# Constants made on chip, one buffer for the normalised values of batch 0, and a new written order, in a fused attention and mixing kernel

## The chip, the cores and the metric

The kernel runs on one core of a Trainium2 chip. The metric is the device time of one execution in microseconds (us); lower is better. The core has a matrix engine (TensorE, PE in the profile, with its weight loads as PEld), a vector engine (VectorE, DVE), an engine for activation functions (ScalarE, ACT), a general engine (GpSimd, POOL) and an engine that issues the transfers (SyncE, SP). Each takes its instructions in the order in which they are written; they wait for each other through semaphores.

## The reference

Four batches of 768 tokens, eight heads of 64. Every token attends to its neighbours at a distance under 16 and to 24 block summaries (the maximum of the keys and the mean of the values of 32 tokens); the result x goes through a gate with sine and cosine, is mixed over the tokens by two 768 by 768 matrices, and through a channel layer:

```python
    scores_l_m = np.where(mask_l, scores_l, -1000000000.0)
    scores_all = np.concatenate([scores_l_m, scores_s], axis=-1)
    scores_all = scores_all - np.max(scores_all, axis=-1, keepdims=True)
    a = np.exp(scores_all)
    a = a / (np.sum(a, axis=-1, keepdims=True) + 1e-09)
    ...
    theta = x @ w_theta
    cos_t, sin_t = (np.cos(theta), np.sin(theta))
    zr = x * cos_t
    zi = x * sin_t
    yr = np.einsum('ts,bsd->btd', w_tok_r, zr)
    yi = np.einsum('ts,bsd->btd', w_tok_i, zi)
    y = yr + yi
    u = x + y
    return (u + np.maximum(u @ w_ch, 0.0)).astype(np.float32)
```

## The kernel before, in words

The work is cut into 24 tiles of 128 tokens, six for each batch, counted here from 0 to 23. A tile goes through these stages, each with a letter that is used below:

- **S**, the scores (line 465, 32 matmuls into two PSUM banks `s`), then eight mask-and-minimum operations on VectorE (L501) and eight exponentials on ScalarE (L505);
- **PT**, the transposes of the exponentials (L514, two halves of four), each copied out of PSUM (L518);
- **AV**, the product with the values (L488, 32 matmuls); the rows are divided by their sums (L526 to L535) into a tile `xn`, three buffers of which go round;
- **X**, the transpose of `xn` (L544) into the one PSUM bank `t`, copied out (L294, L296) into `x`, the transposed x of the whole batch, which has two buffers;
- **TH**, the product with w_theta in four pieces (L569 for the first six tiles, with the weights as plain float32; L574 afterwards, with weights and x split into two parts) into the same bank `t`. The bank is free again when L583 on ScalarE and L587 on VectorE have read it;
- the phase: L583, L586, L587, an absolute value (L592 or L594), and sine and cosine (L598, L599) on ScalarE. Exponential and sine need different tables there, and each switch is an ACT_TABLE_LOAD;
- **Z**, the two products of `xn` with cosine and sine (L609), one for each half of the channels;
- **M**, the mixing (L637): for each batch and half of the channels six steps of four pieces, step i with the Z of tile i. The weights arrive as 64-bit words and are turned into float32 by L353 to L364 (ScalarE or VectorE, then GpSimd or VectorE, then three passes on VectorE).

Before the first tile, a pre-pass makes the block summaries: the maxima on VectorE (L392) and, for batch 0, the value sums as matmuls of `vn` (loaded into a buffer of the tag `x`) with a table of ones (L398). At the very beginning five matmuls on zeros (L331) keep TensorE running while the first transfers arrive. The last stage is the channel layer (L753) with its sums and outputs.

Nothing of the order is found at run time. The function records every operation with its inputs and outputs, and a long table of numbers, `ORDER`, says in which order they are written and which engine takes each (a letter behind the number: a for ScalarE, d for VectorE, g for GpSimd). Durations in the class `Program` and the `cost` of each operation were used when the table was searched; at run time only the table counts.

Three constants come from the host in one array `cst`: the identity for the transposes, three masks of 128 by 118, and the table of ones. They are loaded by three transfers into `cs` and `vt`.

Of the kernel before, what the change touches and what calls it, by code (L numbers as in the profile page):

```python
# [55 lines left out]
12 6d 14 0 13 15 4 7 8 28 18 9 10 11 3 16 20 1 22 19 33a 37g 35a 34a 39 38a 17 36a 40 41 49 5 52 56 42 44 43 46 50 54 47 74  # L56
75a 24 2 68 76d 51 45 53 48 55 170a 169a 21 23 25 26 59 57 164 29 31 27d 77 78 79 69d 70d 32d 71 72 30a 171 80 212 86 165
167 215g 216g 168g 58a 60a 172 175 176 179 173 174 178 81a 177 61 180 183 182 181 217 62a 184 187 185 186 65d 63 66 64d 67d
82g 166g 83 73 84 87a 188 190 199 88g 92 93 266 189a 191a 218 219 220 221 200a 192 224 223 270a 222 225 196a 193a 103a 213
214 94 95 89 85 90 226 91 194 227 197 229 230 228 195d 198d 231 233 232 269g 104g 108a 105 106 201 202 203 204 205 206d 207  # L60
234 236 271 245 235a 237a 109g 272 275 110 274 323a 276 279 246a 238 111 280 281 208a 242a 239a 278 285 284 320 268 322 267
96 389 97 98 321 99 100 101 102 107 112 113 114a 119a 282 240 273 283 243 241d 244d 277 287 286 247 248 249 250 251 115g
324g 116 117 252d 253 120g 209 288 325 290 299 300a 301 302 254a 289a 291a 292 326 118 255 121 210 122 211 123 258 303 256
# [892 lines left out]
```

## Time and profile before

| what | value |
|---|---|
| median of 3 runs | 454.6 us (454.58 to 455.56) |
| time of the profiled execution | 454.5 us |
| span of the instructions in it | 452.7 us |
| granted TensorE clock | 0.999 |
| busy: PE, PEld, DVE, ACT, POOL | 97%, 79%, 74%, 60%, 21% |
| table loads on ScalarE | 24 of 1283 ns |

The span runs from the first instruction to the last; what lies around it is 454.5 - 452.7 = 1.8 us. A row of the timeline gives the start, the duration, the engine, the line and the operation, how many follow each other, and in brackets how long the engine stood idle before it and what ended that. A row of the table of stretches gives the busy time of each engine in that stretch and how many instructions it began.

### The profile page before, as it was taken

The page shows a single profiled execution, that of the slowest core. Times are in us where ns is not written, and L with a number is a line of the kernel's source. Part 1 is how long each engine was busy: PE and PEld are TensorE (multiplying, and loading weights), DVE is VectorE, ACT ScalarE, POOL GpSimd, SP SyncE. Part 2 cuts the span into 40 slices and gives each one's busy share as a digit, 9 for nine tenths or more (in the row PEclk, how much of TensorE's full clock was granted, in tenths as well). Part 3 has the DMA queues.
Part 4 walks back from the last instruction along what each step waited for, and adds up shares of the span by engine and source line. Part 5 has one row for each costly group of instructions (what it writes and reads, how often), then busy time and mean ns, then how long its engine had stood idle before and what let it go on. Part 6 is the DMA issues. An engine that isn't in the chain of part 4 may idle for free.

```text
span 452.7 us, 9375 instructions
## 1 busy us (share of the span) xinstructions
PE 440.9 (97%) x3562; PEld 357.3 (79%) x3562; DVE 336.2 (74%) x930; ACT 271.9 (60%) x595; POOL 94.0 (21%) x98
## 2 busy tenths in 40 slices
PE   8888999999999999999999999999999999999997
PEld 3464655757888888888888888888888878999996
DVE  4799999778576576776638757575654599998996
ACT  2899988887774676966373755366664406526240
POOL 0221204635520103041011100012003100313521
PEclk9999999999999999999999999999999999999999
DMA  8999945323077340412710503101003720000256
GB/s 300 344 332 327 373 154 184 119 60 110 1 227 250 101 119 25 130 42 52 229 37 3 163 1 118 41 3 55 0 2 108 274 85 0 0 19 20 88 186 250
DMA packets 25005, 55.80 MB, mean 123 GB/s; under 512 B 2944, under 2 KB 8320, under 8 KB 24960
## 3 DMA queue, kind: packets, MB, share of 16 engines
q1 hardware_dynamic: 24960, 55.20, 37.4%
q8 instruction: 28, 0.46, 0.4%
q14 instruction: 17, 0.14, 0.1%
HBM read 45.75 MB, written 9.44 MB: 122 GB/s over the span
## 4 chain that ended last, share of the span: by engine, by line
PE 88%; DMA 8%; ACT 2%; DVE 1%; SPq 0%; issue 0%; ACTq 0%
PE m L637 46%; PE t L574 11%; PE c L753 6%; PE m L753 6%; PE pa L488 5%; PE s L465 4%; PE pa L514 4%; PE t L569 3%; DMA wt<-wti 3%; PE t L544 3%; DMA v<-vg 2%; DMA x<-vn 2%; DMA kn<-kT 1%; PE t L753 1%; ACT L598 1%; ACT w L598 0%
## 5 line engine op out<-in xcount | busy, mean ns | idle before, releaser
L637 PE MATMUL m<-wt,zh 128*128 128x512 f32 (+1 forms) x768 | 181.2, 360 | 0.8 <-DVE x L656 0.6
L637 PEld LDWEIGHTS m<-wt,zh 128*128 128x128 f32 x768 | 122.8, 189 | 32.8 <-issue 14.3
L637 PE MATMUL m<-wt,zl 128*128 128x512 f32 x336 | 86.6, 339 | 0.0
L505 ACT ACTIVATE e<-e,st 128x118 f32<-128x118 f32 x192 | 62.9, 388 | 16.3 <-DVE st L501 15.9
L637 PEld LDWEIGHTS m<-wt,zl 128*128 128x128 f32 x336 | 51.2, 188 | 7.4
L501 DVE CUSTOM_DVE_ANT_0 e<-s,cs 128x118 f32<-128x118 f32 x192 | 45.4, 273 | 10.7 <-PE s L465 6.8
L574 PE MATMUL t<-wth,xh 128*128 128x512 f32 x144 | 47.6, 412 | 0.0
L583 ACT ACTIVATE w<-t,bmagic 128x512 f32<-128x512 f32 x24 | 16.5, 688 | 42.2 <-PE t L574 41.3
L448 POOL COPY k<-kn 128x376 f32<-128x376 f32 (+1 forms) x24 | 12.7, 536 | 96.2 <-DVE zl L303 39.8
L488 PEld LDWEIGHTS pa<-v,e 118*64 118x64 f32 x768 | 24.7, 137 | 6.8 <-issue 4.2
L514 PEld LDWEIGHTS pa<-cs,e 128*118 128x118 f32 x192 | 22.7, 136 | 8.9 <-ACT e L505 1.6
L514 PE MATMUL pa<-cs,e 128*118 128x128 f32 x192 | 28.5, 274 | 0.8 <-ACT e L505 0.4
L488 PE MATMUL pa<-v,e 118*64 118x65 f32 x768 | 28.2, 224 | 0.8 <-ACT e L518 0.8
L574 PE MATMUL t<-wth,xl 128*128 128x512 f32 x72 | 28.3, 394 | 0.0
L465 PE MATMUL s<-k,q 64*64 64x118 f32 x768 | 25.3, 268 | 1.3 <-DVE st L527 0.7
L465 PEld LDWEIGHTS s<-k,q 64*64 64x64 f32 x768 | 19.7, 132 | 7.8 <-issue 5.9
L656 DVE TENSOR_TENSOR x<-m,x 128x512 f32<-128x512 f32 (+1 forms) x32 | 16.6, 548 | 11.6 <-PE m L637 11.6
L586 DVE TENSOR_SCALAR w<-w 128x512 f32<-128x512 f32 x19 | 8.6, 451 | 22.4 <-ACT w L583 22.3
L518 DVE COPY e<-pa 118x512 f32<-118x512 f32 x15 | 10.3, 688 | 18.9 <-PE pa L514 18.9
L574 PEld LDWEIGHTS t<-wth,xh 128*128 128x128 f32 x144 | 22.1, 189 | 2.7 <-DVE xl L550 0.3
L303 POOL TENSOR_TENSOR zl<-zb,zh 128x512 fp32r<-128x512 f32 x9 | 11.5, 1289 | 58.6 <-ACT zh L294 31.6
L587 DVE CUSTOM_DVE_ANT_0 w<-t,w 128x512 f32<-128x512 f32 x24 | 16.6, 690 | 8.0 <-POOL w L586 7.4
(168 smaller groups left out, 798.9 us busy)
## 6 DMA issues: line engine op xcount, KB each, us to landing
v<-vg SPq DMA_DIRECT2D x48, 195.0 KB, 4.5
q<-qg SPq DMA_DIRECT2D x24, 256.0 KB, 4.5
kn<-kT SPq DMA_DIRECT2D x6, 798.0 KB, 7.7
wt<-wtr SPq DMA_DIRECT2D x6, 768.0 KB, 10.1
wt<-wti SPq DMA_DIRECT2D x6, 768.0 KB, 11.9
f<-vT SPq DMA_DIRECT2D x12, 384.0 KB, 4.9
cu<-u_scratch SPq DMA_DIRECT2D x8, 384.0 KB, 6.4
out<-cu SPq DMA_DIRECT2D x16, 192.0 KB, 2.5
```

Of the source, the lines that this page charges most:

```text
L465: mm(0.79 * len(pairs) / NP, [lambda p=p, g=g, h=h: nc.tensor.matmul(sc[h].get()[ROW[g], p], q.get()[ROW[h], p, ROW[g]], k.get()[ROW[h], p ...
L488: mm(2 * 0.433 + scores[0] + (0.2 if scores[0] else 0.0), [lambda n=n, g=g, a=a: nc.tensor.matmul(xa[a].get()[ROW[g], n], turned[a].get()[ ...
L501: op({"DVE": 0.205}, lambda eng, n=n: nc.vector.tensor_tensor_reduce(e()[:, n], sc[n % 2].get()[:, 2 * a + n // 2], mask(m), -SCALE, 3.0e3 ...
L505: op({"ACT": 0.288}, lambda eng, n=n: nc.scalar.activation(e()[:, n], e()[:, n], AF.Exp, bias=st.get()[:, n:n + 1], scale=-1.0), [(st, n)] ...
L514: mm(NH * 0.109, [lambda n=n: nc.tensor.transpose(tp.get()[:NK, n], e()[:, n], ident()) for n in range(NH)], [e_ref, (cs, "ident")], [tp], ...
L544: mm(NC * 0.109, [lambda c=c: nc.tensor.transpose(tx.get()[:, c], xn[b, i].get().rearrange("p h d -> p (h d)")[:, c * P:(c + 1) * P], ident())
L574: calls = [lambda t=t, xx=xx, k=k, c=c: nc.tensor.matmul(th.get(), xx.get()[:, c], w_th[c].get()[:, k], start=(c == 0 and t == 0), stop=(c ...
L583: op({"ACT": 0.59}, lambda e: nc.scalar.activation(r(), th.get(), AF.Identity, bias=bmagic.get(), scale=1.0 / TWO_PI), [th, bmagic], [R], due)
L587: op({"DVE": c_dve(DM)}, lambda e: nc.vector._custom_dve(TENSOR_ADD_SAT, out=r(), in0=th.get(), in1=r(), s0=PI_F, s1=-PI_F), [th], [R], due)
L637: nc.tensor.matmul(acc[th](), zz.get()[:, r, cc], w[:, TT[th]], start=(s == 0 and r == 0 and t == 0 and (th == 0 or c == 0)), stop=(s == N ...
L656: op({"DVE": c_dve(nt * P)}, lambda e, u=u, acc=acc: nc.vector.tensor_tensor(u(), acc(), u(), op=ALU.add), [areg] + [(xs, n) for n in rang ...
L753: calls = [lambda k=k, t=t, x=x, y=y: nc.tensor.matmul(to.get(), weights[n][x][0]()[:, k, j * P:(j + 1) * P], operands[n].get()[:, y, k], ...
```

## The change

It has three parts. The lines behind the new code move by 34 to 36: the scores are L499 in the changed kernel, the products with the values L524, the transposes L550 and L580, the first products with w_theta L605, the mixing L673.

First, the constants are made on the chip. The three transfers go; in their place stand six fills (MEMSET, on VectorE or GpSimd) and seven AFFINE_SELECTs on GpSimd, which overwrite what lies off a line or a diagonal:

```diff
-    dma(lambda: sums.get().rearrange("p a n -> p (a n)")[:, :2 * NB - BPT], lambda: cst[:, P + 3 * NK:], (2 * NB - BPT) * 512, [], [sums], 1e6)
-    for k, c in (("mask", slice(P, P + 3 * NK)), ("ident", slice(0, P))):
-        dma(lambda c=c: cs.get()[:, c], lambda c=c: cst[:, c], (c.stop - c.start) * 512, [], [(cs, k)], 1e6)
...
+    def fill(dst, value, n, wr):
+        op({"DVE": c_dve(n, "fast"), "POOL": c_pool(n, False)}, lambda e: V[e].memset(dst(), value), [], [wr], -100.0, port=BOTH)
+
+    def keep(dst, pattern, n, base, step, compare, value, wr):
+        op({"POOL": c_pool(n, False) + 0.1}, lambda e: nc.gpsimd.affine_select(
+            out=dst(), in_=dst(), pattern=pattern, compare_op=compare, fill=value, base=base, channel_multiplier=step), [], [wr], -100.0, port=BOTH)
...
+    fill(lambda: masks(every, slice(0, NB)), math.log(BLK) / SCALE, 3 * NB, (cs, "mask"))
+    fill(lambda: masks(every, slice(NB, NK)), 0.0, 3 * NL, (cs, "mask"))
+    for g in range(2):
+        local = lambda g=g: masks(slice(g * QT, (g + 1) * QT), slice(NB, NK))
+        keep(local, [[0, 3], [1, NL]], 3 * NL, 0, -1, ALU.is_ge, far, (cs, "mask"))
+        keep(local, [[0, 3], [-1, NL]], 3 * NL, 2 * HALO, 1, ALU.is_ge, far, (cs, "mask"))
...
+    fill(flags, 1.0, 2 * NB - BPT, sums)
+    keep(flags, [[-BLK, 2 * NB - BPT]], 2 * NB - BPT, BLK * (NB - BPT), 1, ALU.is_ge, 0.0, sums)
+    keep(flags, [[BLK, 2 * NB - BPT]], 2 * NB - BPT, BLK - 1 - BLK * (NB - BPT), -1, ALU.is_ge, 0.0, sums)
+    fill(lambda: cs.get()[:, 0:P], 0.0, P, (cs, "ident"))
+    keep(lambda: cs.get()[:, 0:P], [[-1, P]], P, 0, 1, ALU.not_equal, 1.0, (cs, "ident"))
```

Second, the six `xn` of batch 0 become six parts of one buffer of the tag `x` (`Part` is a view of a slice; `early` holds the buffer). The tag still has two buffers. The first tile's `vn` has one, `early` the other, the transposed x of batch 0 takes the first one when the sums over `vn` are done, and the transposed x of batch 1 takes that of `early`, when the last Z of batch 0 has read it:

```diff
-        xn[b, i] = Ref(apool, [P, H, D], tag="xn", bufs=K["XNB"])
+        if b == 0 and i == 0:
+            early.append(Ref(tpool, [P, NT, H, D], tag="x", bufs=K["XB"]))
+        xn[b, i] = Ref(apool, [P, H, D], tag="xn", bufs=K["XNB"]) if b else Part(early[0], lambda x, i=i: x[:, i])
```

Third, the table `ORDER` is another one, searched with other durations; a line of each, and one of the durations:

```diff
-12 6d 14 0 13 15 4 7 8 28 18 9 10 11 3 16 20 1 22 19 33a 37g 35a 34a 39 38a 17 36a 40 41 49 5 52 56 42 44 43 46 50 54 47 74
...
-        op({"ACT": 0.16, "DVE": 0.19}, lambda eng: (
+        op({"ACT": 0.16, "DVE": 0.075}, lambda eng: (
```

What the table moves is seen in the order of the built programs, at three places. The first is the opening. On TensorE before, the five matmuls on zeros, the scores of tile 0 (`s`), the sums over `vn` (`x,vt`) and the transposes of tile 0:

```order
L331 MATMUL t<-zb 128x512 x5
L465 MATMUL s_110<-k,q 64x118
...
L398 MATMUL pa_164<-x,vt 24x512 x6
L514 MATMUL pa_173<-cs,e 118x128 x4
L514 MATMUL pa_178<-cs,e 118x128 x4
L465 MATMUL s_200<-k,q 64x118
...
L488 MATMUL pa_247<-v,e 64x65 x8
L488 MATMUL pa_256<-v,e 64x65 x8
L465 MATMUL s_271<-k,q 64x118
```

and now:

```order
L365 MATMUL t<-zb 128x512 x4
L432 MATMUL pa_120<-x,vt 24x512 x2
L499 MATMUL s_129<-k,q 64x118
...
L432 MATMUL pa_120<-x,vt 24x512 x4
L550 MATMUL pa_185<-cs,e 118x128 x4
L550 MATMUL pa_190<-cs,e 118x128 x4
L499 MATMUL s_222<-k,q 64x118
...
L524 MATMUL pa_265<-v,e 64x65 x8
L524 MATMUL pa_274<-v,e 64x65 x8
L365 MATMUL t<-zb 128x512
L499 MATMUL s_300<-k,q 64x118
```

A third of the sums over `vn` now stands ahead of the first scores, and the fifth matmul on zeros behind the first product with the values. GpSimd's first work, which was one copy of keys, is now this (`cs` holds masks and identity, `vt` the table of ones, `k` the keys of a tile; the ISA row is a reload of its library, which stood ahead of the first TENSOR_SCALAR before):

```order
L333 ISA
L333 AFFINE_SELECT vt<-vt 128x44
L330 MEMSET cs 128x3x94
L333 AFFINE_SELECT cs<-cs 64x3x94 x3
L333 AFFINE_SELECT vt<-vt 128x44
L333 AFFINE_SELECT cs<-cs 64x3x94
L330 MEMSET cs 64x15
L482 COPY k<-ks 128x4x24
L482 COPY k<-kn 128x2x94 x3
L482 COPY k<-ks 128x4x24
L482 COPY k<-kn 128x4x94 x2
L333 AFFINE_SELECT cs<-cs 128x128
```

Five of the six copies of keys for tile 0 are now on GpSimd, behind the masks. The second place is ScalarE around the second tile, before (L353 begins the conversion of a piece of w_theta when it has arrived, L518 copies the transposes of tile 1, L294 the transposed x of tile 0):

```order
L505 ACTIVATE e<-e,st 128x118 x4
L353 ACTIVATE xl<-wth_222 128x512
L518 COPY e<-pa_307 118x512
L518 COPY e<-pa_312 118x512
L294 COPY x<-t 128x4x128
```

and now:

```order
L541 ACTIVATE e<-e,st 128x118 x4
L482 COPY k<-kn 128x4x94
L554 COPY e<-pa_322 118x512
L554 COPY e<-pa_327 118x512
L387 ACTIVATE xl<-wth_218 128x512
L305 COPY x<-t 128x4x128
```

The two copies, for which the product AV waits, moved ahead of the conversion. The third place is TensorE where batch 1 begins to overlap the end of batch 0, before (the rows from the transposes of tile 7 to the last mixing step of batch 0's first half; `t<-cs,xn` is X of tile 6, `t<-wth` its TH, `m` the mixing):

```order
L514 MATMUL pa_1138<-cs,e 118x128 x4
L514 MATMUL pa_1143<-cs,e 118x128 x4
L544 MATMUL t<-cs,xn 128x128 x4
L465 MATMUL s_1162<-k,q 64x118
...
L488 MATMUL pa_1188<-v,e 64x65 x8
L488 MATMUL pa_1197<-v,e 64x65 x8
L574 MATMUL t<-wth_911,xh 128x512 x2
L574 MATMUL t<-wth_911,xl 128x512
L574 MATMUL t<-wth_846,xh 128x512 x2
...
L637 MATMUL m_664<-wt,zh 128x512
```

and now:

```order
L550 MATMUL pa_1147<-cs,e 118x128 x4
L550 MATMUL pa_1152<-cs,e 118x128 x4
L499 MATMUL s_1157<-k,q 64x118
...
L580 MATMUL t<-cs,xn 128x128 x4
L524 MATMUL pa_1192<-v,e 64x65 x8
L524 MATMUL pa_1201<-v,e 64x65 x8
L673 MATMUL m_646<-wt,zh 128x512
L673 MATMUL m_648<-wt,zh 128x256
...
L610 MATMUL t<-wth_774,xh 128x512 x2
```

The scores of tile 8 moved ahead of X of tile 6, and TH of tile 6, of which three pieces stood ahead of the mixing, now begins behind its third piece. Over the whole program ScalarE has 32 table loads instead of 24; the eight more all stand behind the first piece of the second half of batch 0's mixing. The numbers of matmuls of each kind are the same.

More of the change, by code (lines that the diff above doesn't have):

```diff
@@ L146, in get, with __init__ @@
         return self.ap
+class Part:
+    def __init__(self, base, cut):
+        self.base, self.cut = base, cut
+    def get(self):
+        return self.cut(self.base.get())
 class Late:
@@ L197, in op @@
                 ref, key = acc if isinstance(acc, tuple) else (acc, None)
[L198 to L206 removed]
+                own = ref.base if isinstance(ref, Part) else ref
+                if isinstance(own, Ref) and own not in o.refs:
+                    if not own.users:
+                        o.allocs.append(own)
+                        self.tags.setdefault((id(own.pool), own.tag), [[], 0])[0].append(own)
+                    else:
+                        first.add(own.users[0])
+                    own.users.append(o)
+                    own.left += 1
+                    o.refs.append(own)
                 st = self.state.setdefault(ref, {})
@@ L264, with attn_moe @@
             T_LEAD=30.0, Z_LEAD=14.0, PRE=2.0, START=34.82, W_LEAD=20.0, WT_LEAD=5.0)
-def attn_moe(tc, qg, vg, kT, vT, vn, wth, wtr, wti, wch, cst, out, tune=TUNE):
+def attn_moe(tc, qg, vg, kT, vT, vn, wth, wtr, wti, wch, out, tune=TUNE):
     nc = tc.nc
@@ L314, in attn_moe @@
     bmagic = Ref(wpool, [P, 1], tag="bmagic")
-    dma(lambda: sums.get().rearrange("p a n -> p (a n)")[:, :2 * NB - BPT], lambda: cst[:, P + 3 * NK:], (2 * NB - BPT) * 512, [], [sums], 1e6)
-    for k, c in (("mask", slice(P, P + 3 * NK)), ("ident", slice(0, P))):
-        dma(lambda c=c: cs.get()[:, c], lambda c=c: cst[:, c], (c.stop - c.start) * 512, [], [(cs, k)], 1e6)
+    masks = lambda rows, cols: cs.get()[rows, P:].rearrange("p (m k) -> p m k", k=NK)[:, :, cols]
+    flags = lambda: sums.get().rearrange("p a n -> p (a n)")[:, :2 * NB - BPT]
+    def fill(dst, value, n, wr):
[3 more added lines that the diff above has]
+            out=dst(), in_=dst(), pattern=pattern, compare_op=compare, fill=value, base=base, channel_multiplier=step), [], [wr], -100.0, port=BOTH)
+    every, far = slice(0, P), -1e9 / SCALE
+    pr.key = ("CONST", 0)
+    fill(lambda: masks(every, slice(0, NB)), math.log(BLK) / SCALE, 3 * NB, (cs, "mask"))
[4 more added lines that the diff above has]
+        keep(local, [[0, 3], [-1, NL]], 3 * NL, 2 * HALO, 1, ALU.is_ge, far, (cs, "mask"))
+    fill(lambda: masks(slice(0, QT), slice(NB, NB + HALO))[:, 0], far, HALO, (cs, "mask"))
+    fill(lambda: masks(slice(QT, P), slice(NB + HALO + QT, NK))[:, 2], far, HALO, (cs, "mask"))
+    fill(flags, 1.0, 2 * NB - BPT, sums)
[3 more added lines that the diff above has]
+    keep(lambda: cs.get()[:, 0:P], [[-1, P]], P, 0, 1, ALU.not_equal, 1.0, (cs, "ident"))
+    pr.key = ("", 0)
     bright = Ref(wpool, [P, 1], tag="bright")
@@ L933, in _layout @@
         "wch": con(moe_w_ch).view(np.int64).reshape(NC, P, DM),
-        "cst": _const(),
     }
```

188 lines of the change are left out of this document (84 added, 104 removed).

## The prediction

> **What bounds the kernel now.** The page gives TensorE 97% of the span, so I first looked for where the other 3% lies. The table of stretches shows it (start and end; then length and the busy time, with the instructions begun, of PE, PEld, DVE, ACT, POOL; granted clock, DMA share, GB/s):
>
> ```profile
> 0.00:50.00 50.00, 43.70 (x388) 23.72 (x389) 39.99 (x146) 37.89 (x89) 10.18 (x20) 1.00 0.99 329
> 50.00:80.00 30.00, 30.00 (x156) 17.52 (x155) 29.53 (x54) 25.84 (x50) 7.92 (x7) 1.00 0.63 218
> 80.00:110.00 30.00, 28.48 (x318) 19.33 (x318) 23.50 (x90) 24.41 (x61) 14.20 (x18) 1.00 0.30 89
> 110.00:345.00 235.00, 234.97 (x2117) 199.71 (x2117) 152.43 (x500) 145.53 (x336) 36.21 (x40) 1.00 0.26 79
> 345.00:400.00 55.00, 54.38 (x307) 47.99 (x306) 43.85 (x71) 21.01 (x33) 10.46 (x8) 1.00 0.29 98
> 400.00:449.00 49.00, 49.00 (x284) 48.94 (x283) 46.16 (x75) 17.20 (x29) 15.02 (x8) 1.00 0.30 109
> 449.00:452.70 3.70, 0.38 (x3) 0.06 (x1) 0.72 (x2) 0.00 (x0) 0.00 (x0) 0.82 0.61 218
> ```
>
> PE is idle for 6.30, 0, 1.52, 0.03, 0.62, 0 and 3.32 us, 11.8 in all. The last 3.32 are the final sum and its transfer, which nothing in the change touches. So this change can win at most 8.5 us, nearly all of it before 110 us, or lose wherever it makes TensorE wait anew. The full stretch from 50 to 80 is a warning: VectorE is busy there for 29.53 of 30 us.
>
> Then the timeline of PE before 46 us, only the rows at which it waits or changes stage (start, duration, engine, line, operation, count, idle time before and its releaser):
>
> ```profile
> 1.46 7.61 PE L331 MATMUL t<-zb 128*128 128x512 f32 x10 [1.46 <-DVE zb L329]
> 10.25 0.63 PE L465 MATMUL s<-k,q 64*64 64x118 f32 x16 [0.61 <-ACT k L448]
> 10.81 3.61 PE L398 MATMUL pa<-x,vt 128*24 128x512 f32 x8
> 14.77 1.90 PE L398 MATMUL pa<-x,vt 128*24 128x512 f32 x4 [0.34 <-DMA x<-vn]
> 16.60 1.40 PE L514 MATMUL pa<-cs,e 128*118 128x128 f32 x8
> 20.95 1.16 PE L465 MATMUL s<-k,q 64*64 64x118 f32 x32 [0.71 <-DVE st L527]
> 24.48 1.46 PE L488 MATMUL pa<-v,e 118*64 118x65 f32 x32 [0.82 <-ACT e L518]
> 31.78 0.65 PE L544 MATMUL t<-cs,xn 128*128 128x128 f32 x4 [0.37 <-DVE w L587]
> 37.71 0.54 PE L514 MATMUL pa<-cs,e 128*118 128x128 f32 x3 [0.41 <-ACT e L505]
> 40.04 0.66 PE L544 MATMUL t<-cs,xn 128*128 128x128 f32 x4 [0.24 <-DVE w L587]
> 41.88 1.12 PE L569 MATMUL t<-xh,x 128*128 128x512 f32 x2 [1.18 <-ACT x L294]
> 44.88 1.34 PE L637 MATMUL m<-wt,zh 128*128 128x512 f32 x3
> ```
>
> **The constants.** The three transfers that go carry little, by the list of DMA issues (KB each, median us to landing):
>
> ```profile
> x<-vn SPq DMA_DIRECT2D x3, 512.0 KB, 7.2
> q<-qg SPq DMA_DIRECT2D x24, 256.0 KB, 4.5
> kn<-kT SPq DMA_DIRECT2D x4, 399.0 KB, 5.0
> cs<-cst SPq DMA_DIRECT2D x1, 177.0 KB, 6.7
> cs<-cst SPq DMA_DIRECT2D x1, 64.0 KB, 7.9
> vt<-cst SPq DMA_DIRECT2D x1, 22.0 KB, 4.6
> ```
>
> 263 KB at 329 GB/s are 0.8 us of transfers, and three issues fewer on SP's queue. The fills on VectorE stand in its gaps before the first keys. The trace has no AFFINE_SELECT. The nearest rows on GpSimd, and the groups of the later steps:
>
> ```profile
> L448 POOL COPY k<-kn 128x376 f32<-128x376 f32 x23 | 12.3, 544 | 87.7 <-DVE zl L303 39.8 <-DVE zb L609 16.3 <-PE s L465 15.1
> L303 POOL TENSOR_TENSOR zl<-zb,zh 128x512 fp32r<-128x512 f32 x9 | 11.5, 1289 | 58.6 <-ACT zh L294 31.6 <-DVE w L609 21.5 <-DVE zh L296 4.8
> L501 DVE CUSTOM_DVE_ANT_0 e<-s,cs 128x118 f32<-128x118 f32 x192 | 45.4, 273 | 10.7 <-PE s L465 6.8 <-PE pa L514 2.3 <-PE pa L488 0.6
> L364 DVE SCALAR_TENSOR_TENSOR xl<-wth,xl 128x512 uint32<-128x512 uint32 x2 | 1.4, 689 | 0.0
> ```
>
> Scaled to 282 elements (3 masks of 94), one select or fill costs 0.41 us by the copy and 0.71 by the two-input operation. GpSimd has five such and three short ones (0.1 to 0.35 each). Begun at 1.5 us, when the fills that they overwrite are through, they end between 3.9 and 6.1. I take the middle, 5. The first to need `vt` are the sums over `vn` at about 8.0, so 2 to 4 us of waiting for transfers cover it: cost zero. Without that cover, by an end after 8.0, every us over is a us on the opening.
>
> **The opening.** TensorE is released by arrivals in both kernels. The last keys of tile 0 stood behind 1874 KB (four of 399, 256, 22); now four of 399 and one third of `vn` make 2108. The 234 KB more are 0.7 us, so the second half of the scores moves from 10.25 to 10.95. `q` now follows them; it is 490 KB behind what had landed by about 8.8, so near 10.3. In the time ahead of that a third of the sums over `vn` (12 matmuls took 3.61 + 1.90) is done, from about 8.0, when four of the five matmuls on zeros are through (five end at 1.46 + 7.61 = 9.07), to 9.9. Scores end at 11.6 instead of 10.9, and 3.7 us of sums remain: the transposes of tile 0 start at 15.3 instead of 16.60, as the wait of 0.34 for `vn` goes too (a piece of w_theta and the masks no longer stand ahead of its last third). But this lead of 1.3 isn't kept. The scores of tile 2 waited 0.71 until VectorE had done the eight masks of tile 1; these now start 1.3 earlier, yet two conversion passes (L364 is 0.69, L359 shorter) now stand among them. I expect 20.4 against 20.95, a lead of **0.55**.
>
> **From 20 to 80 us.** AV of tile 1 waited 0.82 at 24.48 for two copies that stood behind a conversion which itself waited for its weights:
>
> ```profile
> 23.24 0.67 ACT L353 ACTIVATE xl<-wth 128x512 f32<-128x512 f32 x1 [0.75 <-DMA wth<-wth]
> 21.00 0.61 POOL L357 TENSOR_SCALAR xh<-xh 128x512 f32<-128x512 f32 x1 [0.41 <-ACT xh L353]
> ```
>
> Now the copies go first: the wait goes whole, and the lead is 0.55 + 0.82 = 1.4. The waits 0.37, 0.41, 0.24 and 1.18 are 2.2 more, so at the first mixing step the lead could be 3.6. I don't give it all. What stands late next is VectorE: by the rows of the order, four masks (4 x 0.273 = 1.1 us), two conversion passes (1.4) and two divisions more lie ahead of the Z of tile 2, about 3 us with the smaller operations, and between 50 and 80 us VectorE has half a us to spare. How much of that a gap absorbs the trace can't say, so I let half of the 3.6 go there: the lead comes out at **1.8** for everything before 80 us. Bounds: 0, if VectorE takes it all; 4.8, if every wait but the first 1.46 goes (6.30 - 1.46).
>
> **Where batch 1 begins.** The rows from 94 to 104 us are one chain, TH of tile 5 to the first Z that the mixing step waits for:
>
> ```profile
> 94.94 0.69 ACT L583 ACTIVATE w<-t,bmagic 128x512 f32<-128x512 f32 x1 [0.26 <-PE t L569]
> 96.87 0.66 PE L544 MATMUL t<-cs,xn 128*128 128x128 f32 x4 [1.09 <-DVE w L587]
> 98.72 1.28 ACT L598 ACT_TABLE_LOAD   x1
> 99.51 0.74 PE L574 MATMUL t<-wth,xh 128*128 128x512 f32 x2
> 101.29 0.69 DVE L609 TENSOR_TENSOR zh<-xn,w 128x512 f32<-128x512 f32 x1 [0.40 <-ACT w L599]
> 102.04 4.14 PE L637 MATMUL m<-wt,zh 128*128 128x512 f32 x12 [0.19 <-DVE zh L609]
> 365.56 0.73 PE L637 MATMUL m<-wt,zh 128*128 128x256 f32 x3 [0.62 <-DVE x L656]
> ```
>
> The scores of tile 8 (32 such are 1.16 in the row at 20.95) now fill the wait of 1.09. The price is in the second edit: the copy of X of tile 6 into the transposed x of batch 1 must wait for the last Z of batch 0 (which follows the one at 101.29), because that buffer holds `xn`; bank `t` stays taken, and the three pieces of TH of tile 6 (from 99.51, about 2.1 us) that hid sine and cosine can't stand ahead of the mixing. One piece of the mixing step before (a third of 4.14, 1.4) takes their place. So TensorE has 0.7 us less to do inside the chain, and the chain stays at about 7.1 (102.04 - 94.94); it is shorter, down to 6.4, if the table load no longer stands behind the copies of tile 6. So what is won in front is lost behind: **0**, bounds -1.5 and +0.8. Queued behind the waiting copy on ScalarE are its exponentials for tile 8, and for those TensorE's next transposes.
>
> **The rest.** The wait at 365.56 shrinks as more pieces stand ahead of it: **-0.2** (bounds -0.6, 0). The turns between matmul kinds are 256 instead of 276 in the order; by the rows each costs or saves under 0.1 us, both signs, and I count zero. Eight more table loads on ScalarE lie between 110 and 345 us, where there were these:
>
> ```profile
> L598 ACT ACT_TABLE_LOAD x9 | 11.5, 1283 | 0.1
> L505 ACT ACT_TABLE_LOAD x8 | 10.3, 1283 | 1.7 <-DVE st L501 1.5
> ```
>
> 8 x 1.283 = 10.3 us on an engine that idles for 235 - 145.5 = 89 there, while TensorE waited 0.03 in spite of 17 loads. Cost zero, hidden under matmuls; 10.3 if the cover were gone at each.
>
> Sum against the profiled execution, 454.5 (span 452.7 and 1.8 around it; the median is 454.6): 454.5 - 1.8 + 0 - 0.2 = **452.5 us**.
>
> **Rivals.** *VectorE takes the whole lead.* For it: 29.53 of 30. Against: ten idle us on it before 50, into which the work moved forward goes. Then only the 0.2 stays: 454.3.
>
> *More is won.* Every wait goes before 80 and the one before the mixing: 4.8 + 0.2, about 449.5. Against: the new masks and conversions are in the way by the order itself.
>
> *Table loads on the chain (slower).* Place: the phases of batches 1 to 3. The load at 98.72 did stand on the chain to the mixing, between copy and cosine. If three of the eight new ones do so with no matmul ready, 3 x 1.283 = 3.85, and the time is 456.3. It decides from the third on (454.5 + 1.4 is passed by 2.7 loads). Against: 17 were hidden.
>
> *The library arrives late.* GpSimd's reload stands ahead of its first select now, and before ahead of the TENSOR_SCALAR at 21.00, which waited 0.41 and for ScalarE, so the reload cost no more there. If it stalled for long at the start, with the dear price, masks end at 9.7 to 11.1; the key copies behind them (four, 1.3 us) put the scores at 11.0 to 12.4, 1.4 late in the middle: 453.9. In the Trainium skill, "GPSIMD Engine Reference", section 2.1 on instruction dispatch, the first call to a freshly loaded kernel pays about 6 us without a visible instruction, which would give such an end; the 0.41 in this trace speaks against it.
>
> **The numbers.** Forecast, with its own range 450.5 to 453.1 (4.0 to 1.4 won): 0.57. More won: 0.06. VectorE takes it: 0.17. Library: 0.05. Table loads: 0.15. About 0.3%, 1.4 us, is what a measurement here can tell. So faster 0.63, same 0.22, slower 0.15. Range 449.9 to 455.6: up past the two cases of no change and down to most of the larger gain.
>
> **What would show it.** Right: transposes of tile 0 near 15.3, scores of tile 2 near 20.4, no wait at AV of tile 1, less than 4.5 us of PE idle before 50, still full from 50 to 80; selects of 0.4 to 0.7 us, over by 6.1; PE idle near zero from 110 to 345 with 25 loads. Wrong: new waits of PE on `xn`, `w` or `e` between 50 and 345 us, a mixing step that starts later than 102, or first scores after 11.

## The result, and the profile after

The changed kernel took 459.87 us (median of 6, 459.54 to 461.82), the kernel before on the same chip 454.91 us (median of 6). The ratio is 1.0104, with a 95% interval of 1.0084 to 1.0125: the change makes the kernel slower by about 5 us. The forecast was 452.5, with a range up to 455.6. The profiled execution of the changed kernel took 459.54 us with a span of 457.7; that is 5.0 more span than before (452.7), with the same 1.8 around it. The ratios of this document leave out two executions that took far longer than the others of their kernel, one of 1111.51 us (the run below that moves only the second sum) and one of 460.36 us (the kernel before).

The table of stretches of the changed kernel, at the cuts of the prediction (start and end; then length and the busy time, with instructions begun, of PE, PEld, DVE, ACT, POOL; granted clock, DMA share, GB/s):

```profile
0.00:50.00 50.00, 44.65 (x424) 24.41 (x425) 41.02 (x152) 37.81 (x88) 13.74 (x33) 1.00 0.99 334
50.00:80.00 30.00, 28.86 (x122) 16.12 (x121) 28.59 (x57) 23.00 (x43) 4.99 (x7) 1.00 0.50 175
80.00:110.00 30.00, 28.09 (x296) 19.61 (x297) 24.16 (x87) 24.78 (x62) 16.62 (x20) 1.00 0.42 115
110.00:345.00 235.00, 232.03 (x2119) 198.07 (x2116) 152.17 (x493) 154.86 (x346) 33.89 (x39) 0.99 0.25 79
345.00:400.00 55.00, 53.99 (x302) 46.83 (x301) 41.69 (x66) 21.92 (x34) 7.01 (x6) 1.00 0.27 96
400.00:449.00 49.00, 49.00 (x284) 48.93 (x283) 45.39 (x75) 15.43 (x27) 20.79 (x13) 1.00 0.23 82
449.00:457.70 8.70, 5.21 (x31) 4.89 (x29) 4.75 (x9) 0.95 (x2) 1.03 (x1) 1.00 0.74 267
```

PE is now idle for 5.35, 1.14, 1.91, 2.97, 1.01, 0 and 3.49 us, 15.9 in all, against 11.8 before. That is 4.1 of the 5.0 us; the other 0.9 is busy time (441.8 against 440.9), though the matmuls are the same. The opening won 0.95 us of idle time. Every stretch from 50 to 400 lost some, and by far the most was lost where before there was nothing to lose: from 110 to 345 us, 2.97 against 0.03.

The timeline of PE in the changed kernel, only rows at which it waits or changes stage (start, duration, engine, line, operation, count, idle time before and its releaser):

```profile
1.53 5.45 PE L365 MATMUL t<-zb 128*128 128x512 f32 x8 [1.53 <-DVE zb L363]
10.06 1.35 PE L499 MATMUL s<-k,q 64*64 64x118 f32 x32 [1.25 <-POOL k L482]
14.89 1.40 PE L550 MATMUL pa<-cs,e 128*118 128x128 f32 x8
18.44 1.15 PE L524 MATMUL pa<-v,e 118*64 118x65 f32 x30 [0.92 <-DMA v<-vg]
21.02 1.04 PE L499 MATMUL s<-k,q 64*64 64x118 f32 x32 [0.38 <-DVE x L571]
...
66.40 0.63 PE L580 MATMUL t<-cs,x 128*128 128x128 f32 x4 [0.36 <-DVE w L623]
72.52 9.30 PE L673 MATMUL m<-wt,zh 128*128 128x512 f32 x28 [0.77 <-DVE zh L645]
...
86.47 1.16 PE L499 MATMUL s<-k,q 64*64 64x118 f32 x32 [0.84 <-DVE st L537]
99.78 2.85 PE L673 MATMUL m<-wt,zh 128*128 128x512 f32 x8 [0.70 <-DVE zh L645]
...
239.95 0.73 PE L673 MATMUL m<-wt,zh 128*128 128x256 f32 x3 [2.22 <-DVE x L692]
240.52 0.76 PE L673 MATMUL m<-wt,zl 128*128 128x512 f32 x2
241.08 1.05 PE L610 MATMUL t<-wth,xh 128*128 128x512 f32 x2
241.94 0.63 PE L610 MATMUL t<-wth,xl 128*128 128x512 f32 x1
242.36 1.48 PE L673 MATMUL m<-wt,zh 128*128 128x512 f32 x4
243.64 0.69 PE L673 MATMUL m<-wt,zl 128*128 128x512 f32 x2
244.18 0.85 PE L673 MATMUL m<-wt,zh 128*128 128x512 f32 x4
244.87 0.51 PE L673 MATMUL m<-wt,zl 128*128 128x512 f32 x2
245.22 0.62 PE L610 MATMUL t<-wth,xh 128*128 128x512 f32 x2
245.67 0.40 PE L610 MATMUL t<-wth,xl 128*128 128x512 f32 x1
...
370.18 0.74 PE L673 MATMUL m<-wt,zh 128*128 128x256 f32 x3 [0.96 <-DVE x L692]
```

One wait stands out: 2.22 us at 239.95, for the sum of the mixing on VectorE (L692). And behind it the matmuls are slow. Four mixing pieces take 1.48 at 242.36 and 0.85 at 244.18; two pieces with w_theta 1.05 at 241.08 and 0.62 at 245.22. Over the five rows from 240.52 to 243.64, each against its like from 244.18 on, that is 0.25 + 0.43 + 0.23 + 0.63 + 0.18 = 1.72 us. The table of stretches for PE alone (busy time, clock, DMA share, GB/s) has the reason, the granted clock:

```profile
240.00:244.00 4.00, 4.00 (x13) 0.58 0.00 0
```

So in this execution this place costs 2.2 of waiting and 1.7 of slow clock, 3.9 of the 5.0 us. Why the sum came late is seen in VectorE's timeline of the changed kernel at that place,

```profile
235.56 0.76 DVE L571 TENSOR_TENSOR xn<-pa,st 128x256 f32<-128x256 f32 x2
236.23 1.74 DVE L426 TENSOR_REDUCE ks<-kn 128x48 f32<-128x1536 f32 x1
237.89 0.68 DVE L692 TENSOR_TENSOR x<-m,x 128x512 f32<-128x512 f32 x1
238.49 0.68 DVE L314 TENSOR_TENSOR zl<-w,zh 128x512 fp32r<-128x512 f32 x1
239.08 0.27 DVE L537 CUSTOM_DVE_ANT_0 e<-s,cs 128x118 f32<-128x118 f32 x1
...
239.48 0.42 DVE L692 TENSOR_TENSOR x<-m,x 128x256 f32<-128x256 f32 x1
```

beside the one of the kernel before:

```profile
237.62 1.02 DVE L656 TENSOR_TENSOR x<-m,x 128x256 f32<-128x256 f32 x2 [6.16 <-PE m L637]
238.56 1.75 DVE L392 TENSOR_REDUCE ks<-kn 128x48 f32<-128x1536 f32 x1
```

These are the two sums at the end of a mixing step of batch 1 (second half of the channels). Before, VectorE stood idle for 6.16 us until the matmuls were done, took both sums at once and only then a maximum over keys for the next batch (L392, 1.75). In the new order the key maximum (L426, 1.74) stands ahead of both sums, and a subtraction and two masks between them. TensorE's next mixing pieces write into the PSUM bank that the second sum still has to read, so they wait for all of it.

### The profile page after: what moved, and what is told of

Its sections match the earlier page's. It is cut to its first block, busy times and chain, and to the rows that moved or that the text cites. A ratio compares the mean times of both kernels' runs of the same rounds, so it can differ in the third digit from the quotient of the medians.

```text
span 457.7 us, 9398 instructions
## 1 busy us (share of the span) xinstructions
PE 441.8 (97%) x3562; PEld 358.9 (78%) x3562; DVE 337.8 (74%) x935; ACT 278.8 (61%) x599; POOL 98.1 (21%) x116
## 4 chain that ended last, share of the span: by engine, by line
PE 78%; DVE 10%; DMA 4%; ACT 4%; issue 1%; SPq 1%; POOL 0%; DVEq 0%; ACTq 0%; POOLq 0%
PE m L673 40%; PE t L610 11%; PE c L789 6%; PE m L789 6%; PE pa L524 4%; DMA v<-vg 4%; PE s L499 4%; PE pa L550 4%; PE t L580 2%; DVE f L395 2%; PE t L605 2%; DVE wt L398 2%; DVE e L537 1%; SPq L299 1%; PE t L789 1%
## 5 line engine op out<-in xcount | busy, mean ns | idle before, releaser
L673 PE MATMUL m<-wt,zh 128*128 128x512 f32 (+1 forms) x768 | 181.2, 360 | 4.9 <-DVE x L692 3.5
L673 PEld LDWEIGHTS m<-wt,zh 128*128 128x128 f32 x768 | 123.9, 189 | 36.9 <-issue 12.3
L673 PE MATMUL m<-wt,zl 128*128 128x512 f32 x336 | 87.5, 341 | 0.0
L673 PEld LDWEIGHTS m<-wt,zl 128*128 128x128 f32 x336 | 51.7, 189 | 7.5
L314 POOL TENSOR_TENSOR zl<-zb,zh 128x512 fp32r<-128x512 f32 x11 | 14.8, 1359 | 71.5 <-DVE zb L645 41.8
L524 PEld LDWEIGHTS pa<-v,e 118*64 118x64 f32 x768 | 24.8, 137 | 6.3 <-issue 2.9
L524 PE MATMUL pa<-v,e 118*64 118x65 f32 x768 | 28.3, 224 | 1.3 <-DMA v<-vg 1.3
L499 PE MATMUL s<-k,q 64*64 64x118 f32 x768 | 25.3, 267 | 2.6 <-POOL k L482 1.3
L499 PEld LDWEIGHTS s<-k,q 64*64 64x64 f32 x768 | 19.7, 132 | 10.1 <-issue 4.3
L645 DVE TENSOR_TENSOR w<-xn,w 128x512 f32<-128x512 f32 x18 | 12.4, 689 | 20.5 <-ACT w L635 20.4
L550 PEld LDWEIGHTS pa<-cs,e 128*118 128x118 f32 x192 | 21.8, 136 | 6.7 <-issue 2.7
L692 DVE TENSOR_TENSOR x<-m,x 128x512 f32<-128x512 f32 (+1 forms) x32 | 17.2, 552 | 13.1 <-PE m L673 13.1
L550 PE MATMUL pa<-cs,e 128*118 128x128 f32 x192 | 25.8, 274 | 0.8 <-DVE xn L571 0.5
L482 POOL COPY k<-kn 128x376 f32<-128x376 f32 (+1 forms) x24 | 11.0, 479 | 72.1 <-DVE zh L645 20.1
L554 DVE COPY e<-pa 118x512 f32<-118x512 f32 x19 | 12.8, 687 | 13.9 <-PE pa L550 13.9
```

The source lines that it names most:

```text
L314: lambda e: V[e].tensor_tensor(dst(), src(), hi().bitcast(F32), op=ALU.subtract), reads, writes, due, port=BOTH)
L499: mm(0.79 * len(pairs) / NP, [lambda p=p, g=g, h=h: nc.tensor.matmul(sc[h].get()[ROW[g], p], q.get()[ROW[h], p, ROW[g]], k.get()[ROW[h], p ...
L524: mm(2 * 0.433 + scores[0] + (0.2 if scores[0] else 0.0), [lambda n=n, g=g, a=a: nc.tensor.matmul(xa[a].get()[ROW[g], n], turned[a].get()[ ...
L550: mm(NH * 0.109, [lambda n=n: nc.tensor.transpose(tp.get()[:NK, n], e()[:, n], ident()) for n in range(NH)], [e_ref, (cs, "ident")], [tp], ...
L673: nc.tensor.matmul(acc[th](), zz.get()[:, r, cc], w[:, TT[th]], start=(s == 0 and r == 0 and t == 0 and (th == 0 or c == 0)), stop=(s == N ...
L692: op({"DVE": c_dve(nt * P)}, lambda e, u=u, acc=acc: nc.vector.tensor_tensor(u(), acc(), u(), op=ALU.add), [areg] + [(xs, n) for n in rang ...
```

## The experiments

Most edits move a few numbers of the order table; which operations they are is said beside each. Each group of runs had its own runs of the kernel before beside it, and they are compared through the ratio to those.

### The two sums

The theory was that the wait at 239.95 comes from the key maximum ahead of the sums, and costs what stands ahead. In the first run both sums (1187 and 1189) go ahead of the key maximum (1115); in the second only the second sum goes, directly behind the first, so that the key maximum stays ahead of both.

```diff
-1079d 1080 1081d 1084d 1115 1187 1178d 1146 1144 1189 1203 1141 1117
+1079d 1080 1081d 1084d 1187 1189 1115 1178d 1146 1144 1203 1141 1117
```

> The changed kernel, with one move on VectorE: the first two sums of the mixing of batch 1, second half, go ahead of the key maximum of 1.74 us behind which they stood at 236.2 to 239.9 us. Theory A (a place in VectorE's queue): the wait of 2.22 us and the slow clock behind it (0.58 over about 4 us, some 1.6 us) both go: 459.9 - 3.8 = 456.1 us, 455.6 to 456.6, no wait of the mixing near 238 and no dip of the clock. Rival B (ScalarE's eight more table loads make everything on VectorE late): the wait only moves to what is now behind, the key maximum and the masks of the next tile; over 458.4 us.

```diff
-1079d 1080 1081d 1084d 1115 1187 1178d 1146 1144 1189 1203 1141 1117
+1079d 1080 1081d 1084d 1115 1187 1189 1178d 1146 1144 1203 1141 1117
```

> The changed kernel with half of that move: both sums stay behind the key maximum, but the second goes directly behind the first, ahead of one subtraction and two masks (0.68 + 0.4 us). Theory A: the wait shrinks from 2.2 to about 1.2 us. If the clock falls only behind a wait longer than those which left it at 1.00 (0.84 to 1.25 us in both kernels), the dip goes too: 459.9 - 1.05 - 1.6 = 457.2 us. If the clock falls all the same: 458.8. Rival B: 459.3 or more.

With both sums first the ratio is 1.0039 (1.0018 to 1.0060), and the wait is gone: from 110 to 345 us PE is busy for 234.25 of 235.

```profile
110.00:345.00 235.00, 234.25 (x2138) 200.18 (x2137) 153.88 (x496) 157.32 (x351) 33.96 (x39) 1.00 0.26 80
```

With the second sum alone moved the ratio is 1.0073 (1.0045 to 1.0101), and the timeline of PE shows a wait of half the size, with the clock at full speed behind it:

```profile
239.35 0.74 PE L673 MATMUL m<-wt,zh 128*128 128x256 f32 x3 [1.22 <-DVE x L692]
239.93 0.51 PE L673 MATMUL m<-wt,zl 128*128 128x512 f32 x2
```

The wait follows what stands ahead of the sums: 2.22 with key maximum, subtraction and masks, 1.22 with the key maximum alone, none with nothing. In time, the two sums are worth 0.65% of 455, 3.0 us of the 5.0 (4.0 of 5.8 by the second measurement of the changed kernel, which follows). The wait alone is 2.2 and with the slow clock 3.9; the intervals don't tell these apart.

The changed kernel was also run again:

> The changed kernel once more, beside the others of this set. All theories: 1.0084 to 1.0125 of the kernel before, as it was measured first. It tells how often the slow clock behind the wait of 2.2 us at 240 us comes: if in every execution, the mean granted clock is 0.996 or lower in all of them; if in some, 0.996 in some and 1.000 in others, the latter about 1.7 us shorter.

It came out at 1.0127 (1.0103 to 1.0150), with the same wait: PE busy for 12.78 of the 15 us from 235 to 250, at a clock of 0.89. So the place is no accident of one profile.

### The constants

Here the three transfers of constants are put back into the changed kernel (the fills and selects go, all else stays), and in the other run the first part of the change is put into the kernel before.

```diff
-    fill(lambda: masks(every, slice(0, NB)), math.log(BLK) / SCALE, 3 * NB, (cs, "mask"))
...
-    keep(lambda: cs.get()[:, 0:P], [[-1, P]], P, 0, 1, ALU.not_equal, 1.0, (cs, "ident"))
+    for k, c in (("mask", slice(P, P + 3 * NK)), ("ident", slice(0, P))):
+        dma(lambda c=c: cs.get()[:, c], lambda c=c: cst[:, c], (c.stop - c.start) * 512, [], [(cs, k)], 1e6)
```

> The changed kernel and its order, but the constants come by the three transfers again (table of ones behind the first third of the block values, masks behind q, identity behind the last third). Prediction's step (constants cost and win nothing): 459.9, within 0.7. If the chip-made constants are worth their 0.8 us of transfers: up to 460.7. If they delay GpSimd's key copies and so the first scores: 458.7 to 459.2.

> The kernel before and its order, with the first part of the change alone: constants made on chip at the beginning. Prediction's step: 454.9, within 0.7, the first scores wait for the keys as before. If the transfers that go are worth their time: 454.1. If the selects hold GpSimd's one key copy of tile 0 or VectorE's maxima: over 455.6.

The first gives 1.0123 (1.0091 to 1.0156), no better than the changed kernel, with the same wait of 2.23 us for the sum. The second gives 0.9994 (0.9969 to 1.0019). Constants made on the chip cost nothing and win nothing that can be measured. The groups of GpSimd in the changed kernel give the price of a large select, 0.43 us:

```profile
L333 POOL TENSOR_SCALAR_AFFINE_SELECT cs<-cs 64x282 f32<-64x282 f32 x4 | 1.7, 432 | 0.3
```

### The one buffer

The kernel before with the second part of the change alone. The buffer forces two moves in its order: the copy of X of tile 6 stands behind the last Z of batch 0, and three pieces of TH of tile 6 behind three mixing pieces.

```diff
-        xn[b, i] = Ref(apool, [P, H, D], tag="xn", bufs=K["XNB"])
+        if b == 0 and i == 0:
+            early.append(Ref(tpool, [P, NT, H, D], tag="x", bufs=K["XB"]))
+        xn[b, i] = Ref(apool, [P, H, D], tag="xn", bufs=K["XNB"]) if b else Part(early[0], lambda x, i=i: x[:, i])
```

> The kernel before with the second part of the change alone: one buffer for the normalised values of batch 0. Its order is kept but for two things that the buffer forces: the copy of X of tile 6 into the transposed x of batch 1 goes behind the last Z of batch 0, and three pieces of TH of tile 6 behind three pieces of the mixing step that they covered. Prediction's step (the 2.1 us of cover are missing, and nothing is put in their place here): TensorE waits 2.3 to 2.6 ahead of that mixing step, 457.0 to 457.7; if a wait over 2 us slows the clock as at 240 us in the changed kernel, 1.6 more, up to 459.3. If the buffer costs nothing by itself: 454.9, within 0.7.

The ratio is 1.0073 (1.0051 to 1.0095). PE is idle for 4.13 us from 80 to 110 instead of 1.52, and the timeline shows where:

```profile
98.65 0.66 PE L557 MATMUL t<-cs,xn 128*128 128x128 f32 x4 [1.10 <-DVE w L600]
103.32 4.14 PE L650 MATMUL m<-wt,zh 128*128 128x512 f32 x12 [1.96 <-DVE zh L622]
108.29 0.73 PE L587 MATMUL t<-wth,xh 128*128 128x512 f32 x2 [0.84 <-ACT x L305]
```

The wait for the first Z grew from 0.19 to 1.96, since the pieces of TH that hid sine and cosine can't stand ahead of the mixing, and the copy of X of tile 6 is waited for (0.84). So the buffer alone has a price of some 2.6 us at this place, and the changed order covers nearly all of it (1.91 idle, 0.4 more than before). The other half, the changed order with `xn` in buffers of its own, wasn't run.

### The small waits behind 110 us, and those before

To the run with both sums first, three more moves, all of sums of the mixing: the one near 197 us goes behind a division that frees a bank, one near 285 behind the last matmul into its own bank, and one near 367 four places forward. A second run adds four moves between 60 and 100 us: a phase ahead of a weight conversion, the last conversion behind the Z of tile 3, and two mixing pieces put as filling into later waits. The first of the three late moves is this one:

```diff
-993 962 961 965 972 995 927 988g 1002g 928d 966
+993 962 961 965 972 927 988g 1002g 928d 995 966
```

> The kernel with the sums first (1.8 us over before), with only the three moves behind 110 us out of the seven of the last set (waits of 0.47 at 197, 0.29 at 285, 0.34 of 0.96 at 367). Theory A holds where VectorE has time to spare (152 of 235 us busy from 110 to 345): the waits go and are not paid back, 1.1 us less, ratio 1.0015. Rival C (they come back here too): 1.004.

> The kernel with the sums first (ratio 1.0039 to before, so 1.8 us slower), and seven more moves, one for each wait that TensorE still has behind 60 us: the phase step that frees bank t ahead of a weight conversion (0.39 us at 67), the last conversion behind Z of tile 3 (0.76 at 73), one piece of the mixing ahead of the scores of tile 7 (0.84 at 87), one more ahead of the last mixing step of batch 0 (0.70 at 100), a division ahead of a sum (0.47 at 197), a sum behind the last piece into its bank (0.29 at 285), a cast behind a sum (0.34 of 0.96 at 367). Theory A (each wait is the place of one instruction in a queue): all go, 3.8 us, so 2.0 us under the kernel before: ratio 0.9956. Rival C (VectorE and the chain of sine and cosine are full there, a wait that is removed comes back behind): the waits before 110 us, 2.7, come back, ratio 1.001 to 1.004.

The three late moves give 1.0023 (1.0005 to 1.0042): from 110 to 345 us all that was lost is won back, PE is busy for 235.00 of 235, with all the new table loads. The seven moves give 1.0058 (1.0026 to 1.0090), no better than the two sums alone (1.0039). The waits between 60 and 100 didn't go, they came back elsewhere:

```profile
73.91 5.43 PE L673 MATMUL m<-wt,zh 128*128 128x512 f32 x16 [0.70 <-DVE zh L645]
...
84.86 0.65 PE L550 MATMUL pa<-cs,e 128*118 128x128 f32 x4 [0.84 <-ACT vs L455]
```

These and the others in that stretch name VectorE, directly or by one step more (the copy on ScalarE follows a sum of values on VectorE). That raised the question whether VectorE sets the pace up to 80 us, the rival that the prediction gave 0.17.

### Does VectorE set the pace before 80 us?

The direct test adds work to it: four fills of 128 by 512 that nobody reads, at 33 us, to the run with both sums first.

```diff
+    for _ in range(4):
+        op({"DVE": 0.4}, lambda e: nc.vector.memset(idle.get(), 0.0), [], [idle], port=BOTH)
...
-119g 330 104 277 278 105
+119g 1991 1992 1993 1994 330 104 277 278 105
```

> The kernel with the sums first, and four fills of 128x512 on VectorE at about 30 us that nothing needs (0.35 to 0.48 us each, 1.4 to 1.9 in all). Theory E (VectorE is the bound from 25 to 80 us): the whole dose is in the time, 1.4 to 1.9 us, ratio 1.007 to 1.008. If TensorE is the bound there and VectorE has gaps that take it: 1.004, no change.

The ratio went from 1.0039 to 1.0105 (1.0080 to 1.0130), 3.0 us for a dose that lasts 2.4 (from 32.99 to 35.37). VectorE's timeline has the first of the fills, PE's the wait that followed:

```profile
32.99 0.48 DVE L918 MEMSET zb<- 128x512 f32 x1
```

```profile
38.62 1.06 PE L550 MATMUL pa<-cs,e 128*118 128x128 f32 x8 [1.95 <-DVE x L571]
39.52 1.47 PE L605 MATMUL t<-xl,x 128*128 128x512 f32 x2
40.91 1.85 PE L499 MATMUL s<-k,q 64*64 64x118 f32 x32
```

X of tile 4 began at 70.11 us instead of 67.03, 3.1 later. That isn't the dose alone. This execution was 0.3 late ahead of it (33.84 against 33.55); then TensorE waited 1.95, and its matmuls behind that wait ran at a clock of 0.50 from 40 to 42 us, so the first mixing step began 3.9 late (44.08 against 40.16), of which 0.8 was made up by 67 us. The four executions with a mean clock of 0.999 or more, in which no such slow stretch shows, took 458.46 to 459.16 us, which is 1.8 to 2.5 us more than the ratio without the dose gives. So most of the dose, or all of it, is in the time: at 33 us VectorE holds TensorE back. The run doesn't test VectorE between 50 and 80 us, where TensorE is nearly full too and would hand on a delay by itself.

The opposite test takes work from it: one limiting step (L391, a minimum and a maximum over 128 by 768) of each of the last four converted weight pieces goes from VectorE to GpSimd, in the run with the late waits removed. In the third of the following runs the kernel before gets the same assignment; there three of these steps move, and an earlier one that the changed order already had on GpSimd. The second adds the two mixing pieces as filling.

```diff
-155d 152 156 153 320 157 159a 369 362a 160d 158 161 370d 162 164a 359a 165d 163 169a 371 166 170d 167 171
+155g 152 156 153 320 157 159a 369 362a 160g 158 161 370d 162 164a 359a 165g 163 169a 371 166 170g 167 171
```

> The kernel with the sums first and without the three late waits (1.0023 of before), with the limiting of four pieces of mixing weights between 58 and 68 us (0.55 us each on VectorE) given to GpSimd, which stands idle from 58 to 78 us. Theory E (VectorE's work sets the time up to 80 us): 1.5 to 1.9 us less, ratio 0.9985. Rival (the chain of transfers, scores and sine sets it, VectorE is only full because work is ready early): 1.002.

> The same, with two pieces of the mixing put behind the products with the values of tile 5 and ahead of the last mixing step of batch 0, where TensorE waited 0.84 and 0.70 us. Theory E: with VectorE ahead these fills now count, 1.0 to 1.5 us more, ratio 0.995 to 0.9965, faster than both kernels. Rival: they are paid back as before, no better than the run beside it.

> The kernel before, with the same four operations given to GpSimd. TensorE has no wait there from 50 to 80 us, and the next (0.24, 1.09, 0.19 us) hang on the chain of tile 5. Theory E as said of the changed order alone: within 0.3 us, ratio 0.999 to 1.001. If VectorE's amount sets the time in this order too: 1.0 us or more less, ratio under 0.998.

The ratios are 1.0072 (1.0050 to 1.0094), 1.0073 (1.0048 to 1.0099) and 1.0038 (1.0016 to 1.0060): all three lost, the first two against the 1.0023 that they started from. The timeline of GpSimd in the first of them shows what happened there:

```profile
56.48 0.83 POOL L391 TENSOR_SCALAR f<-f 128x768 f32<-128x768 f32 x1 [3.88 <-DVE wt L398]
58.06 1.52 POOL L391 TENSOR_SCALAR f<-f 128x768 f32<-128x768 f32 x1 [0.75 <-DVE f L393]
```

The moved operations took 1.52 us, the same ones that were on GpSimd all along 0.83, and VectorE waited 0.72 for each of three of them (the first at 59.62), 2.2 in all, as much as the move took off it (four times 0.55). The steps of a converted piece form a chain, each waiting for the last, so a longer step on another engine is no relief. In the kernel before the moved operations were no slower (two in 1.62), but there too VectorE waited for them (0.46 at 54.73, 1.26 at 62.87), and TensorE's wait for X of tile 4 was 0.57 (at 68.71) where it had been none. These runs don't show what VectorE with truly less to do would give; that stays open.

### The order of the first transfers

Two runs with both sums first also change the opening: one lets the values of tiles 0 and 1 go ahead of pieces of w_theta (the wait of 0.92 at 18.44 is for them), the other lets all keys and queries go ahead of `vn`. A further run joins the first of these with the seven moves.

> The kernel with the sums first, and on SyncE the four transfers of v for tiles 0 and 1 ahead of the pieces of w_theta between which they stood. Theory A: the products with the values wait no longer for v (1.08, 0.51 and 0.36 us): 1.5 to 1.9 us less, ratio near 1.000. Rival D (the prediction's own step for the opening: the scores of tile 2 wait for the masks on VectorE anyway): only the part that the lead over VectorE leaves, 0.5 us, ratio 1.003.

> The kernel with the sums first, with all keys and q of tile 0 loaded ahead of the block values again, and the scores of tile 0 on TensorE ahead of the sums over vn. Theory E (from its first mask on to 80 us VectorE sets the time, so the first scores do): the masks start at 11.0 instead of 11.6, 0.6 us less in the end, ratio 1.0025. Rival (TensorE and the transfers set it): 1.004 or, since TensorE idles longer ahead of the scores, up to 1.006.

> Both groups of moves together. Theory A: 3.8 + 1.7 = 5.5 us less than the kernel with the sums first, ratio 0.992, 3.7 us faster than before. Rival C or D: the gains don't add, ratio over 0.997.

The ratios are 1.0043 (1.0015 to 1.0072), 1.0090 (1.0067 to 1.0113) and 1.0072 (1.0044 to 1.0101). In the first the waits for values at tiles 0 and 1 went, and this came in their place on PE:

```profile
17.00 1.04 PE L499 MATMUL s<-k,q 64*64 64x118 f32 x32 [0.73 <-DVE xl L395]
21.17 1.04 PE L499 MATMUL s<-k,q 64*64 64x118 f32 x32 [0.99 <-DVE st L564]
23.75 1.00 PE L550 MATMUL pa<-cs,e 128*118 128x128 f32 x4 [0.96 <-ACT e L541]
```

In the second the masks of tile 0 began 0.6 us earlier (10.81 against 11.44), but the transposes of tile 0 stood behind all sums over `vn` and began at 15.84 instead of 14.75. No run beat the kernel before; the nearest is that kernel with the constants made on chip, which equals it.

## Why the prediction was wrong

Against its own sum the profile has this, in us of span:

| step | forecast | measured | from |
|---|---|---|---|
| everything before 80 | -1.8 | -0.57 | value sums of batch 1 at 81.65 instead of 82.22 |
| start of batch 1 | 0 | +0.39 | idle 1.91 - 1.52 |
| 110 to 345 | 0 | +4.66 | idle 2.97 - 0.03, slow clock 1.72 |
| wait near 365 | -0.2 | +0.39 | idle 1.01 - 0.62 |
| end | 0 | +0.17 | idle 3.49 - 3.32 |
| sum | -2.0 | +5.04 | the spans: 457.7 - 452.7 = 5.0 |

**The step that failed is "The rest".** It looked behind 110 us at the wait near 365, the turns between matmul kinds and the table loads, and by these alone gave the stretch a cost of zero. What the order table moved on VectorE there wasn't looked at. The kernel before was full on PE from 110 to 345 with VectorE busy for only 152 of 235 us; I took that as slack that any order keeps. But the slack there was in the order, not in the busy time: two sums that before stood ahead of a 1.75 us reduction now stand behind it, and TensorE's next pieces need their bank. The runs with the sums moved show that this place holds 3.0 of the 5.0 us, and three smaller waits for VectorE hold the rest of the idle time there (the ratio falls from 1.0039 to 1.0023 without them, which is within the intervals). The prediction's last paragraph named the right kind of sign (new waits of PE between 50 and 345 us), on the wrong tiles.

**Table loads.** The cost of zero was right, and the rival that ended on the slower side, eight more loads on the chain, was wrong. There are 25 between 110 and 345 now, and where the three late moves were made the stretch is full with all of them:

```profile
L634 ACT ACT_TABLE_LOAD x13 | 16.7, 1283 | 0.1
L541 ACT ACT_TABLE_LOAD x12 | 15.4, 1283 | 2.7 <-DVE st L537 2.6
```

So the loss came from a mechanism that no rival had, and the sign that the prediction had named for being right there held by half: the loads are 25, but PE is idle for 2.97 us and not near zero.

**The lead before 80 us** was mis-sized: 0.6 instead of 1.8, and it may be none. Five profiles share this order up to 80 us, and in them the value sums of batch 1 begin between 81.65 (the one in the table) and 82.94, in the middle at 82.28, against 82.22 in the one profile of the kernel before. Its first part came out right or better: transposes of tile 0 at 14.89 (15.3 forecast). Then it failed twice. The product with the values of tile 0 waited 0.92 for a transfer of `v`, which the working hadn't looked at since no row of before waited for it; and the scores of tile 2 came at 21.02, not 20.4. The transfer alone doesn't explain that: in the run with the values first this wait is gone, and the scores of tile 2 come at 21.17, after 0.99 of waiting for VectorE. And of what was left before 66 us (0.57 + 0.36 + 0.77 = 1.7), VectorE took two thirds with the waits of 0.36 and 0.77 at 66.40 and 72.52. I had let half of the 3.6 go there on the strength of 29.53 busy of 30; the five profiles speak for the rival "VectorE takes the whole lead" as the better reading of that row, and the dose shows VectorE as the bound at 33 us, though it doesn't test the stretch from 50 to 80. Even the 0.57 isn't won from waits: idle time before 80 rose by 0.2 (5.35 + 1.14 against 6.30), so PE's busy time up to there fell by 0.76 in this profile. That goes with faster first matmuls (eight on zeros in 5.45 us, ten in 7.61 before), which no run tests.

**The start of batch 1** came out as worked: forecast 0, bounds -1.5 and +0.8, measured +0.4. The buffer's price was seen rightly (2.1 us of cover lost; alone it costs 2.6 there), and so was the wait of 1.09 that the scores of tile 8 fill, but a new one of 0.84 for masks (86.47) took its place.

**The constants** were right at zero: the selects of 282 elements took 0.43 (0.41 to 0.71 expected), and those of the masks ended before 5.2 (5 expected). Only the sign for the first scores came out a little differently in this profile: they begin at 10.06 and wait for copies of the keys on GpSimd, not for `q`. In the second profile of the same kernel they begin at 10.28 and do wait for `q` (1.34). The rival of a late library was wrong. In the Trainium skill, "GPSIMD Engine Reference", section 2.1, the first call to a freshly loaded kernel pays about 6 us; here GpSimd's first select stood at 1.71 us and no idle time of that kind follows:

```profile
1.71 0.22 POOL L333 TENSOR_SCALAR_AFFINE_SELECT vt<-vt 128x44 f32<-128x44 f32 x1 [1.18 <-DVE cs L330]
...
5.08 0.11 POOL L330 MEMSET cs<- 64x15 f32 x1 [0.59 <-DVE cs L330]
```

**What stays open.** With nearly all waits behind 110 us removed the kernel is still 0.23% over before, 1.0 us. Its waits between 66 and 101 us and those for values in the opening are candidates; every attempt to move them away only moved them. And the share of the slow clock isn't settled: of the ten executions of the changed kernel five show a mean clock of 0.998 or more and are no faster (459.61 to 461.82) than the five at 0.996 (459.54 to 460.96).

## What to carry to other kernels

When a table or a planner reorders a kernel, compare the order on every engine along the whole program, above all where the busy time says that nothing is tight: look for a long instruction that now stands ahead of one whose result frees a PSUM bank, and price it with its duration. An engine that is busy for nearly all of a stretch can take up a lead that is won ahead of it, so such a lead is worth nothing until it has been followed through, and one profile isn't enough to tell a lead of half a microsecond. And a step that goes to an idle engine wins only if it isn't on a chain and if the two engines don't slow each other.

## What of the hardware was unexpected

A wait of about 2 us can halve TensorE's clock for some 3.4 us (an estimate from the mean of 0.58 over the 4 us from 240, with 0.50 from 242 to 244). It was so behind waits of 2.22 (the changed kernel), 2.23 (constants by transfer), 1.95 (the dose: clock 0.50 from 40 to 42) and 1.82 (the opening with constants by transfer). It wasn't so behind 1.22 (second sum moved), nor behind 1.96 (one buffer alone), and not even behind 2.53 (all keys first, the scores of tile 0 at 9.31: clock 1.00 from 8 to 20 us). So the length of a wait alone doesn't decide it. The Trainium skill, "TensorE: Matmul & The Clock Gate", Part 1, puts the slow state behind an idle window of about 3.4 us that runs freely; no wait of TensorE ahead of its last sums was that long in these runs (2.53 at most), and the half clock came after little more than half of it (1.82).

GpSimd's limiting of 128 by 768 took 0.83 us before 57 us and 1.52 afterwards in one and the same run. It goes with what VectorE does beside it. Each of the four of 1.52 has a conversion pass with two inputs from the on-chip memory beside it (L395 or L398, 0.96 us, the first at 57.94) for its first 0.84 us; those of 0.83 have none. In the kernel before with the moved steps a pair of them took 1.62 at 61.22 while VectorE all but stood still. And there VectorE lost once: a pass of one input, begun at 68.86 when GpSimd was already at work, took 1.17 instead of 0.55. So one of the two seems to wait for the other; how, and through what, no run shows.
